# Transposing q and k in fp32 through two 64-row halves of the TensorE array

## The chip, the cores and the metric

The kernel runs on one NeuronCore of one Trainium2 chip. Its engines are TensorE (PE in the profile; PEld is its loading of weights), VectorE (DVE), ScalarE (ACT), GpSimd (POOL) and SyncE (SP), which here only issues DMAs. The metric is the device time of one execution in microseconds (us); lower is better. The two runs shown took 213.46 and 213.87 us, median 213.67 us.

## What is computed

Two blocks follow each other. The first is causal attention over 4 batches x 8 heads, 768 tokens, head size 64, in which each query sees only 6 chunks of 32 keys. The chunks are chosen by an upper bound on the scores:

```python
k_min = np.min(k_chunks, axis=3); k_max = np.max(k_chunks, axis=3)      # 24 chunks of 32 keys
ub = np.sum(np.maximum(q[:, :, :, None, :] * k_min[:, :, None, :, :],
                       q[:, :, :, None, :] * k_max[:, :, None, :, :]), axis=-1)
ub = np.where(causal, ub, -1000000000.0)
top_chunks = np.argsort(ub, axis=-1)[..., -6:]
scores = scale * np.matmul(q, k.transpose(0, 1, 3, 2))                 # kept where chosen and causal
attn = softmax(scores); out = np.matmul(attn, v)
```

The second is a gated feed-forward block on the 4 x 768 x 512 result `x`:

```python
h = gelu_tanh(x @ w_in); u, v = h[..., :512], h[..., 512:]
v_n = (v - mean(v)) / sqrt(var(v) + 1e-6) * g_ln
v_s = np.einsum('ts,bsd->btd', w_sg, v_n) + b_sg[None, :, None]
return x + (u * v_s) @ w_out
```

## The kernel before

**The pairs.** The 32 heads are handled as 16 pairs, p = 0 to 15; a pair's two heads (i = 0, 1) lie side by side, so that 128 partitions hold 2 x 64 features. Four pairs make a batch, and the feed-forward block of a batch (`moe_h`, `moe_g`) follows when its four pairs are done. While the pairs of one batch are scored, the pairs of the next are prepared.

**Preparing a pair** (`prep`, L1079) has these operations, under the names that the program gives them:

- `ktr` (L574): k arrives as 128 tokens x 128 (head, feature) in fp32, six such blocks. TensorE transposes each: the block is the stationary operand, an fp32 identity of 128 x 128 the moving one (`rows_T`, L547 to L553; the matmuls are on L550). Three blocks, one half (`hf`) of the 768 tokens, go into one PSUM bank as 128 x 384 fp32. A pair has two such operations.
- `kmm` (L578): VectorE reduces a bank to minimum and maximum over each 32 keys, 12 values per half. Two per half. `wsub` (L597) subtracts the minima from the maxima.
- `kev` (L585): the bank is copied as bf16 into `KA`, by ScalarE (by VectorE for pair 2). One copy per half for pairs 0 to 3 and 8 to 15, two copies of 64 partitions for pairs 4 to 7.
- `qtr` (L604), `qev` (L606): the same for q, two operations of three transposes, and one copy to `qT` in fp32 per half (VectorE for pairs 2 and 3). `rel` (L616) is a ReLU of `qT` (ScalarE from pair 4 on), `qcast` (L625) a cast to bf16 on GpSimd.
- `ub` (L660, L707): the bounds, 32 fp32 matmuls on tiles of 64 rows x 32 columns of the array, for one pair (p < 4) or two. Into two banks. Then `utr`, `m8`, `dn`, `dt` on VectorE pick the sixth largest bound and make the mask.

**Scoring a pair.** For pairs 0 to 3 `sc` (L834, L840) runs on tiles of 64 rows x 128 columns, one head in each half of the array's rows. From pair 4 on `sc` (L795) uses the whole array. `exp` (L801, L849) is ScalarE's exponential of up to 1024 columns. `pv` and `pvd` (L879, L885) multiply with v, `xs` (L897) scales the result. `xtr` (L919) transposes the attention's output for the feed-forward block, whose TensorE operations are `hv` (L943), `hu` (L962), `pt` (L1014) and `ou` (L1047); `os` (L1056) adds x on VectorE.

**PSUM.** There are eight banks of 2 KB per partition. Two pairs of banks (`PSC`) serve the scores alone; four single banks (`PSG`, slots 0 to 3) serve all else. From pair 6 on, `ktr`, `qtr` and `ub` may use slots 0 and 1 only (L558, L603, L695); `pv` has slots 2 and 3 (L875); `hv` and `hu` of the first three batches use all four (L939, L958). An operation that takes a slot waits for every operation on the slot's previous tile (L114 to L120), and operations of different engines on one tile wait for each other (L69 to L71).

**The order.** Every engine works through a fixed list. `Program.op` numbers the operations as the program text creates them; `TABLE` (L1133) holds, for each engine, the numbers in the order in which it issues them, further the slot of each PSUM tile, and `filler`: how many idle matmuls (L381, of a zero tile, to keep TensorE at work) it issues ahead of the wait of a given operation. The table was found by a search ahead of time; its costs are the functions at L232 to L258. TensorE's list is in order: an operation that waits for a slot holds up all that stand behind it. SP's queue of DMAs has such a list too.

Of the kernel before, what the change touches and what calls it, by code (L numbers as in the profile page):

```python
# [256 lines left out]
def dmac(issue=530):  # L257
    return issue, issue  # L258


def _build(nc, ctx, q, k, v, w_in, g_ln, w_sg, b_sg, w_out, out):
# [18 lines left out]
    TG = S // 2  # L280
# [42 lines left out]
    WSB = 1  # L323
    WSC = "pool"
# [152 lines left out]
    def wsg_load(j):  # L477
# [4 lines left out]
        if WSB:  # L482
# [3 lines left out]
            elif WSC == "dve":  # L486
                P.op("dve", lambda d: d.tensor_copy(sb, dst), dve(S, rate=2), ("wsc", j), port=True,
                     reads=[("stg", j % 4)] + names, writes=[("stb", j % 4)])
            else:
                P.op("act", lambda d: d.activation(sb, dst, ACTF.Copy), act(S), ("wsc", j),  # L490
                     reads=[("stg", j % 4)] + names, writes=[("stb", j % 4)])
            t = ps_g.tile((0, 1))
# [61 lines left out]

    def kside(p):
        s, w = p % NKS, p % NW
# [33 lines left out]
        if p >= KSPR:  # L590
            P.op("sp", lambda e: e.dma_start(KA[w][1][64:128, :], KA[w][0][64:128, :]), dmac(640), ("kcp", p),
                 reads=[("KA", w, 0, h) for h in range(2)], writes=[("KA", w, 1, h) for h in range(2)] + [("KI", w, 0)],
                 dma=f"kcp{w}", xfer=450)
            P.op("sp", lambda e: e.dma_start(KA[w][0][64:128, :], INDF[64:128, :]), dmac(640), ("kin", p),
                 reads=["INDF"], writes=[("KI", w, 0)], dma=f"kin{w}", xfer=450)
        ws = [("W", w, m, hf) for m in range(2) for hf in range(2)]
        P.op("dve", lambda d: d.tensor_tensor(W[w][:, 1, 0:NC], W[w][:, 1, 0:NC], W[w][:, 0, 0:NC],  # L597
                                              op=ALU.subtract), dve(24), ("wsub", p), port=True, reads=ws, writes=ws)
# [513 lines left out]
    for p in range(4, NP + 4):  # L1112
# [152 lines left out]
```

## Time and profile before

| what | us |
|---|---|
| median of the two runs (213.46, 213.87) | 213.67 |
| the profiled execution's own time | 213.85 |
| its span, first to last instruction | 212.1 |
| TensorE matmuls busy | 203.4 |
| VectorE busy | 184.1 |
| ScalarE busy | 158.5 |
| GpSimd busy | 88.8 |

The span is 1.75 us shorter than the execution's own time, for what lies before the first and after the last instruction. Busy times count the union of an engine's instructions. A matmul's record runs from its issue to the modelled end, about 0.16 us after its last column went in, so records of matmuls that follow each other overlap, and a short gap of TensorE hides in them. The granted clock of TensorE is 0.999 over the span.

### The profile page before, as it was taken

To read this page: it belongs to the slowest core of one execution; us is meant where nothing else is said; L and a number is where in the kernel's file an instruction comes from. 1 tells how busy PE (TensorE), PEld (TensorE's weight loads), DVE (VectorE), ACT (ScalarE), POOL (GpSimd) and SP (SyncE) were. 2 spreads that over 40 slices of the span, in tenths; PEclk is the share of its full clock that TensorE was granted. 3 is DMA by queue.
4 is the path that set the end of the run, shared out by engine and by line. 5 is a ranking of instruction groups with operands and counts; after the bars stand their busy time and mean duration, and the time that the engine had idled before them with its cause. 6 is when DMAs were issued, how large, how long until landed. Compare 5 with 4: busy or idle time off the path is not lost.

```text
span 212.1 us, 5923 instructions
## 1 busy us (share of the span) xinstructions
PE 203.4 (96%) x2326; PEld 134.0 (63%) x2326; DVE 184.1 (87%) x537; ACT 158.5 (75%) x246; POOL 88.8 (42%) x119
## 2 busy tenths in 40 slices
PE   7989999889999999999999999999999999999993
PEld 3646677644767577776456767779646668545552
DVE  2999999879999899898799999899897887788894
ACT  2468999987599779998949989999977868256000
POOL 8424697795262645474121456465502311002000
PEclk9999999999999999999999999999999999999999
DMA  7999999992989998898989988826320007412007
GB/s 152 218 219 254 212 237 336 338 306 68 221 225 231 215 273 205 194 211 189 230 201 220 207 165 220 224 79 149 59 61 3 3 0 97 129 47 105 2 33 264
DMA packets 91339, 36.07 MB, mean 170 GB/s; under 512 B 84144, under 2 KB 86448, under 8 KB 91312
## 3 DMA queue, kind: packets, MB, share of 16 engines
q1 hardware_dynamic: 91024, 35.31, 73.7%
q8 instruction: 18, 0.29, 0.6%
q10 hardware_dynamic: 288, 0.39, 0.5%
q14 instruction: 9, 0.07, 0.1%
HBM read 24.77 MB, written 6.29 MB: 146 GB/s over the span
## 4 chain that ended last, share of the span: by engine, by line
PE 63%; DVE 23%; ACT 9%; issue 2%; POOL 1%; DVEq 0%
PE PSG L1014 15%; PE PSC L795 11%; PE PSG L1047 9%; PE PSG L943 7%; DVE W L578 6%; PE PSG L962 6%; ACT E L801 5%; PE PSG L550 5%; PE PSG L879 4%; DVE vhat L996 3%; DVE XS L897 2%; PE PSG L707 2%; ACT KA L450 2%; PE PSC L382 2%; PE PSG L885 2%
## 5 line engine op out<-in xcount | busy, mean ns | idle before, releaser
L801 ACT ACTIVATE E<-PSC 128x1024 bf16<-128x1024 f32 (+1 forms) x72 | 62.9, 917 | 7.8 <-PE PSC L795 7.6
L795 PE MATMUL PSC<-QA,KA 128*128 128x128 bf16 (+2 forms) x336 | 37.5, 246 | 0.4
L578 DVE TENSOR_REDUCE W<-PSG 128x12 f32<-128x384 f32 x64 | 32.7, 547 | 3.8 <-PE PSG L550 3.6
L1014 PE MATMUL PSG<-wsgT,vhat 128*128 128x384 bf16 x192 | 34.5, 326 | 0.4 <-DVE vhat L996 0.2
L806 POOL TENSOR_SCALAR_AFFINE_SELECT E<-E 128x768 bf16<-128x768 bf16 x24 | 21.1, 878 | 32.3 <-ACT E L801 31.9
L625 POOL CAST QA<-qT 64x768 bf16<-64x768 f32 (+1 forms) x28 | 24.1, 859 | 15.9 <-ACT qT L450 10.0
L795 PEld LDWEIGHTS PSC<-QA,KA 128*128 128x128 bf16 x336 | 24.1, 98 | 8.4 <-ACT E L801 2.4
L1014 PEld LDWEIGHTS PSG<-wsgT,vhat 128*128 128x128 bf16 x192 | 17.9, 98 | 12.5 <-ACT uT L968 1.3
L1047 PE MATMUL PSG<-woutb,uT 128*128 128x512 bf16 (+1 forms) x100 | 23.7, 371 | 0.0
L962 PE MATMUL PSG<-xT,winb 128*128 128x384 bf16 x128 | 23.6, 326 | 0.0
L1031 DVE SCALAR_TENSOR_TENSOR PSG<-PSG,glnT,bsgbc 128x384 f32<-128x384 f32 x32 | 19.7, 619 | 4.1 <-PE PSG L1014 3.9
L849 ACT ACTIVATE E<-PSC 128x1024 bf16<-128x1024 f32 (+3 forms) x26 | 21.2, 866 | 2.4 <-PE PSC L840 2.1
L943 PE MATMUL PSG<-winb,xT 128*128 128x512 bf16 x96 | 22.1, 379 | 0.6 <-issue 0.6
L968 ACT ACTIVATE uT<-PSG 128x384 bf16<-128x384 f32 x32 | 15.1, 490 | 10.0 <-PE PSG L962 9.7
L450 ACT ACTIVATE KA<-PSG 128x384 bf16<-128x384 f32 (+1 forms) x38 | 18.3, 492 | 3.7 <-DVE W L578 3.3
L879 PE MATMUL PSG<-vx,E 128*128 128x65 bf16 x480 | 19.9, 194 | 1.0 <-DVE XS L897 0.6
L635 POOL CAST vx<-vn 128x768 bf16<-128x768 f32 x16 | 13.3, 836 | 17.8 <-DMA vn<-in_v_dram 13.4
L879 PEld LDWEIGHTS PSG<-vx,E 128*128 128x128 bf16 x480 | 17.6, 97 | 3.6 <-DVE XS L897 1.5
L948 ACT ACTIVATE vgb<-PSG 128x512 f32<-128x512 f32 x24 | 13.2, 599 | 7.2 <-PE PSG L943 7.0
L1035 DVE TENSOR_TENSOR uT<-PSG,uT 128x384 bf16<-128x384 f32 x32 | 17.7, 555 | 0.9
L897 DVE TENSOR_TENSOR XS<-PSG,rden 128x384 bf16<-128x384 f32 x32 | 17.7, 554 | 0.9
L952 DVE BATCH_NORM_STATS2 stats<-vgb 128x6 f32<-128x512 f32 x24 | 15.8, 685 | 2.6 <-ACT vgb L948 2.5
(88 smaller groups left out, 328.8 us busy)
## 6 DMA issues: line engine op xcount, KB each, us to landing
kn<-in_k_dram SPq DMA_DIRECT2D x32, 192.0 KB, 4.6
qn<-in_q_dram SPq DMA_DIRECT2D x32, 192.0 KB, 4.5
vn<-in_v_dram SPq DMA_DIRECT2D x12, 384.0 KB, 5.2
out_dram<-osb SPq DMA_DIRECT2D x18, 256.0 KB, 2.4
vn<-in_v_dram SPq DMA_DIRECT2D x8, 192.0 KB, 4.8
uT<-in_moe_w_sg_dram SPq DMA_DIRECT2D x4, 384.0 KB, 6.2
vgb<-in_moe_w_in_dram SPq DMA_DIRECT2D x3, 512.0 KB, 6.1
KA<-INDF SPq DMA_DIRECT2D x12, 96.0 KB, 2.6
```

Source lines behind the costliest of these rows:

```text
L450: P.op("act", lambda e: e.activation(dst(), src(), ACTF.Copy), act(n), tag, reads=reads, writes=writes, ps=ps, shift=shift)
L578: P.op("dve", lambda d, m=m, op=op, src=src, h0=h0, h1=h1: d.tensor_reduce(W[w][:, m, 12 * h0:12 * h1].rearrange("p (h c) -> p h c", h=h1 ...
L625: P.op("pool", lambda g, i=i, r0=r0, r1=r1: g.tensor_copy(QA[w][i or 0][r0:r1, :], qT[r][r0:r1, :]), gps(S, 250 if i == 1 else 150), ("qca ...
L795: r = e.matmul(t.ap()[:, o:o + n], KA[w][i][:, 128 * kb:128 * kb + 128], QA[w][i][:, q0:q0 + n], start=True, stop=True)
L801: P.op("act", lambda e, t=t, c0=c0, c1=c1, i=i: e.activation(E[es][:, i, c0:c1], t.ap()[:, 0:c1 - c0], ACTF.Exp, scale=SCALE), act(c1 - c0 ...
L849: P.op("act", lambda e, t=t, c0=c0, c1=c1, n=n: e.activation(E[es][:, :, c0:c1], t.ap().rearrange("p (i x) -> p i x", i=2)[:, :, 0:n], ACT ...
L879: r = e.matmul(t.ap()[:, 65 * (qb - q0):65 * (qb - q0) + 65], E[es][:, i, at[kb, qb]:at[kb, qb] + 128], vx[w][:, kb, i, :], start=x == 0, ...
L897: P.op("dve", lambda d, pv3=pv3, nq=nq, rs=rs, q0=q0, q1=q1: d.tensor_tensor(XS[:, b % 2, hh // 2, q0:q1, i * DH:(i + 1) * DH], pv3()[:, : ...
L943: r = e.matmul(t.ap()[:, 0:F], xT[s][:, dk, 128 * qt:128 * qt + 128], winb[:, dk, F:DFF], start=(dk == 0), stop=(dk == NDK - 1), skip_grou ...
L962: r = e.matmul(t.ap()[:, 0:TG], winb[:, dk, 128 * fb:128 * fb + 128], xT[s][:, dk, TG * tg:TG * tg + TG], start=(dk == 0), stop=(dk == NDK ...
L1014: r = e.matmul(t.ap()[:, 0:TG], vhat[s][:, sb, 128 * fb:128 * fb + 128], wsgT[:, sb, TG * tg:TG * tg + TG], start=(sb == 0), stop=(sb == N ...
L1047: r = e.matmul(t.ap()[:, 0:n1 - n0], gT[s][:, fb, 128 * qt:128 * qt + 128], woutb[:, fb, n0:n1], start=(fb == 0), stop=(fb == NF - 1))
```

## The change

In place of two operations of three transposes there is one of twelve. A block of 128 tokens is cut in two halves of 64 tokens, which lie on partitions 0 to 63 and 64 to 127. Each half is the stationary operand (64 rows x 128 columns) of a transpose of its own, with an identity of 64 x 64 as the moving operand, so that it occupies one half of the array's rows. The half r goes into bank r: a bank now holds, for each of the six blocks, its 64 tokens r, and not three whole blocks. The readers follow: `kmm` writes its 12 values in steps (two of every four), and the copies to `KA` and `qT` write runs of 64 tokens, every second one (`by64`, `flat64`). Sizes and number of the reductions, the copies and the DMAs are as before.

`ktr` and `qtr` each take two slots at once and each is marked done when its last transpose is done. There are 32 TensorE operations fewer in the list (405 before, 373 after), so all numbers are new, and the table is new too, from a search of 12 seconds. `WSD` is off and does nothing.

```diff
@@
+    WSD = 0
+    TR2 = 1
@@
+    def rows_T2(src, ts):
+        def tr(e):
+            for j in range(NT):
+                for r in range(2):
+                    res = e.matmul(ts[r].ap()[:, 64 * j:64 * j + 64],
+                                   src[64 * r:64 * r + 64, j].rearrange("p i d -> p (i d)"),
+                                   identF[64 * r:64 * r + 64, 64 * r:64 * r + 64], is_transpose=True)
+            return res
+        return tr
+
+    def by64(ap, r):
+        return ap.rearrange("p (j r x) -> p j r x", r=2, x=64)[:, :, r, :]
+
+    def flat64(ap):
+        return ap[:, 0:TG].rearrange("p (j x) -> p j x", x=64)
+
+    def kside2(p):
+        s, w = p % NKS, p % NW
+        ts = [ps_g.tile((0, 1, 2, 3) if p < 6 else (0, 1)) for _ in range(2)]
+        P.op("pe", rows_T2(kn[s], ts), pe32(*[64] * NT), ("ktr", p, 0), mode=1,
+             reads=[("kn", s, h, i) for h in range(2) for i in range(2)] + ["identF"], writes=ts, alloc=tuple(ts))
+        for h, t in enumerate(ts):
+            for m, op in ((0, ALU.min), (1, ALU.max)):
+                P.op("dve", lambda d, m=m, op=op, t=t, h=h: d.tensor_reduce(
+                    W[w][:, m, 0:NC].rearrange("p (j r c) -> p j r c", r=2, c=2)[:, :, h, :],
+                    t.ap()[:, 0:TG].rearrange("p (j c x) -> p j c x", c=2, x=32), axis=AX.X, op=op),
+                    dve(TG), ("kmm", p, h, m), reads=[t, ("W0", w)], writes=[("W", w, m, h)], ps=[t])
+            for i in (None,) if p < HALF or p >= KSPR else range(2):
+                r0, r1 = (0, 128) if i is None else (64 * i, 64 * i + 64)
+                evac("dve" if p in KDVE else "act", lambda h=h, i=i, r0=r0, r1=r1: by64(KA[w][i or 0][r0:r1, :], h),
+                     lambda t=t, r0=r0, r1=r1: flat64(t.ap()[r0:r1]), TG, ("kev", p, h), [t],
+                     [("KA", w, i or 0, h)] + ([("KI", w, 0)] if p >= KSPR else []), [t], shift=(i == 1))
+        kcopies(p, w)
...
     def kside(p):
+        if TR2:
+            kside2(p)
+            return
...
     def qside(p):
         s, w, r = p % NQS, p % NW, p % NR
+        if TR2:
+            ts = [ps_g.tile((0, 1, 2, 3) if p < 6 else (0, 1)) for _ in range(2)]
+            P.op("pe", rows_T2(qn[s], ts), pe32(*[64] * NT), ("qtr", p, 0), mode=1,
+                 reads=[("qn", s, h, i) for h in range(2) for i in range(2)] + ["identF"], writes=ts, alloc=tuple(ts))
         for hf in range(2):
+            if TR2:
+                t = ts[hf]
+                evac("dve" if p in QDVE else "act", lambda hf=hf: by64(qT[r][:], hf), lambda t=t: flat64(t.ap()), TG,
+                     ("qev", p, hf), [t], [("qT", r, hf)], [t])
+                continue
...
     "filler": (
-        "45:7 54:4 84:4 "),
+        "45:8 53:5 78:6 59:1 "),
```

`kcopies` holds, unchanged, the two DMAs and the subtraction that stood at the end of `kside` (L590 to L598). With the numbers written as names (pair, and half where there are halves), these stretches of the lists matter below. TensorE's new list after batch 0's third `ou`, and again in batch 1:

```
ub.6 sc.5.1.1 sc.4.1.2 ou.0.0  qtr.8  ou.0.5  qtr.10 ktr.9  pv.4.1 pvd.4.1 ou.0.4 pv.4.0 pvd.4.0  qtr.9  ou.0.3 sc.6.0.0  ktr.8
sc.11.0.1  qtr.15  pvd.9.1 sc.11.1.0 pvd.9.0 sc.11.1.2  ktr.14  sc.11.1.1 sc.11.0.0 ou.1.3 ou.1.5 pv.10.0 pvd.10.0 sc.12.0.0  ktr.15
```

The old list has at the first of these places: `ou.0.0 qtr.10.1 sc.4.0.2 ou.0.5 qtr.8.0 sc.4.1.2 qtr.10.0 sc.5.1.2 qtr.8.1 sc.5.1.1 qtr.9.0 ktr.9.0 ou.0.4 ...`. ScalarE's new list at the first place: `qev.8.1 qev.8.0 rel.8 qev.10.0 qev.10.1 rel.10 kev.9.0 kev.9.1 qev.9.1 qev.9.0 rel.9 exp.6.0.0`. VectorE's at the second: `rcp.9.1 kmm.14 xs.9.1 rcp.9.0 kmm.14 xs.9.0 kmm.14 os.1.3 kmm.14 os.1.5`. At the start of the attention of batch 0 VectorE's new list has one of the copies of `IND` (L412) ahead of the first reduction. Ahead of `ub.4` and batch 0's feed-forward block, three of the four `xtr` of that batch now stand before `ub.4`; in the old list two of the four did.

Counted over TensorE's whole list, neighbouring operations change between the array whole, in 64 x 128 tiles and in 64 x 32 tiles 49 times before and 76 times after. Up to and into `ub.4` there are 38 such changes before and 27 after; behind it 11 and 49, for the ten pairs 6 to 15 have 20 transposing operations there, of which only `qtr.10` and `ktr.9` are neighbours.

More of the change, by code (lines that the diff above doesn't have):

```diff
@@ L491, in wsg_load @@
                      reads=[("stg", j % 4)] + names, writes=[("stb", j % 4)])
+            if WSD:
+                P.op("sp", lambda e: e.dma_start_transpose(wsgT[:, :, 128 * j:128 * j + 128], sb), dmac(1300), ("wst", j),
+                     reads=[("stb", j % 4)] + [("vhat", 0, x) for x in range(NT)],
+                     writes=[("wsgT", j, hf) for hf in range(2)], dma=f"wt{j}", xfer=900)
+                return
             t = ps_g.tile((0, 1))
@@ new lines, in kcopies @@
+    def kcopies(p, w):
+        if p >= KSPR:
+            P.op("sp", lambda e: e.dma_start(KA[w][1][64:128, :], KA[w][0][64:128, :]), dmac(640), ("kcp", p),
+                 reads=[("KA", w, 0, h) for h in range(2)], writes=[("KA", w, 1, h) for h in range(2)] + [("KI", w, 0)],
+                 dma=f"kcp{w}", xfer=450)
+            P.op("sp", lambda e: e.dma_start(KA[w][0][64:128, :], INDF[64:128, :]), dmac(640), ("kin", p),
+                 reads=["INDF"], writes=[("KI", w, 0)], dma=f"kin{w}", xfer=450)
+        ws = [("W", w, m, hf) for m in range(2) for hf in range(2)]
+        P.op("dve", lambda d: d.tensor_tensor(W[w][:, 1, 0:NC], W[w][:, 1, 0:NC], W[w][:, 0, 0:NC],
+                                              op=ALU.subtract), dve(24), ("wsub", p), port=True, reads=ws, writes=ws)
@@ L589, in kside @@
                      [("KA", w, i or 0, h) for h in hs] + ([("KI", w, 0)] if p >= KSPR else []), ts, shift=(i == 1))
[L590 to L598, printed above, removed]
+        kcopies(p, w)
     def qside(p):
         s, w, r = p % NQS, p % NW, p % NR
+        if TR2:
+            ts = [ps_g.tile((0, 1, 2, 3) if p < 6 else (0, 1)) for _ in range(2)]
+            P.op("pe", rows_T2(qn[s], ts), pe32(*[64] * NT), ("qtr", p, 0), mode=1,
+                 reads=[("qn", s, h, i) for h in range(2) for i in range(2)] + ["identF"], writes=ts, alloc=tuple(ts))
         for hf in range(2):
+            if TR2:
[3 more added lines that the diff above has]
+                continue
             t = ps_g.tile((0, 1, 2, 3) if p < 6 else (0, 1))
```

9 lines of the change are left out of this document (5 added, 4 removed), and 116 rows, old and new, of the table TABLE.

## The prediction

> **What bounds the kernel now.** I read the page first (spans, shares, the chain of waits), then busy time in six stretches, for all and for the transposes alone, then single lines and tiles, last TensorE's timeline at a few places. From the page:
>
> ```profile
> span 212.1 us, 5923 instructions
> PE 203.4 (96%) x2326; PEld 134.0 (63%) x2326; DVE 184.1 (87%) x537; ACT 158.5 (75%) x246; POOL 88.8 (42%) x119
> ...
> PE 63%; DVE 23%; ACT 9%; issue 2%; POOL 1%; DVEq 0%
> ```
>
> TensorE has most of the chain, but not everywhere. The stretches (length; busy PE, PEld, DVE, ACT, POOL; clock, DMA) say where:
>
> ```profile
> 0.00:46.00 46.00, 41.74 (x648) 28.00 (x648) 38.88 (x126) 35.30 (x57) 30.75 (x52) 1.00 1.10 254
> 46.00:81.00 35.00, 34.73 (x278) 22.27 (x279) 32.75 (x101) 28.35 (x48) 18.08 (x23) 1.00 0.95 204
> 81.00:97.00 16.00, 15.36 (x268) 11.99 (x265) 14.47 (x51) 15.74 (x25) 9.80 (x13) 1.00 0.90 204
> 97.00:113.00 16.00, 15.77 (x139) 8.82 (x140) 13.91 (x39) 11.47 (x22) 2.84 (x3) 1.00 0.96 212
> 113.00:152.00 39.00, 39.00 (x544) 29.52 (x544) 35.46 (x115) 37.07 (x53) 20.65 (x25) 1.00 0.78 168
> ```
>
> From 81 to 97 ScalarE works 15.74 of 16 us and sets the pace. From 46 to 81 and from 113 on it is TensorE, with VectorE close behind. In the first 46 us VectorE has 38.88 us, and most of it is chain:
>
> ```profile
> 9.52 1.94 DVE W L578 x4
> ...
> 29.25 1.40 DVE W L578 x3
> ...
> 44.67 0.78 PE PSG L919 x12
> ```
>
> The fp32 transposes alone, in the same stretches (PE's busy time and count first):
>
> ```profile
> 0.00:46.00 46.00, 11.89 (x72) 8.23 (x72) 1.00 1.10 254
> 46.00:81.00 35.00, 6.63 (x42) 4.86 (x42) 1.00 0.95 204
> 81.00:97.00 16.00, 4.23 (x27) 2.87 (x27) 1.00 0.90 204
> 97.00:113.00 16.00, 2.08 (x12) 1.33 (x12) 1.00 0.96 212
> 113.00:152.00 39.00, 6.26 (x39) 4.53 (x39) 1.00 0.78 168
> ```
>
> 72 of 192 lie in VectorE's stage, 27 in ScalarE's, 93 where TensorE counts. The busy times overstate them, since records overlap. What one costs comes from its line and two places of the timeline:
>
> ```profile
> L550 PE MATMUL PSG<-identF,kn x96: 272/273/475, 4.6 to 145.8; 128*128 128x128 f32 x96
> ...
> 70.04 0.38 PE L550 MATMUL PSG<-identF,qn 128*128 128x128 f32 x2
> ...
> 70.20 0.66 PE PSG L550 x6
> ```
>
> A record is 272 ns, two take 0.38 us, so the second starts 109 ns after the first; six take 0.66 us of the chain, 6 x 109 = 654 ns.
>
> **The change part by part. Transposing.** A half block has 64 columns to move where the whole one had 128. 109 ns for 128 are 0.83 ns each and 2.5 over, so 64 take 56 ns if both halves run at once. That halves run at once is seen in the scores of pairs 0 to 3, which use the same tiles in bf16:
>
> ```profile
> 18.80 0.23 PE L834 MATMUL PSC<-QA,KA 64*128 64x128 bf16 x2
> ...
> L840 PE MATMUL PSC<-Dt,IND 64*128 64x128 bf16 x40 | 3.7, 216 | 0.0
> ```
>
> The two matmuls together take 0.23 us, one alone 216 ns. Nothing was loaded ahead for them, and both are longer by little more than 10 ns: the weights of the second half did not wait for the first's. So twelve transposes are six rounds. A round can't be shorter than the load of the next fp32 weights, which shows where none was loaded ahead:
>
> ```profile
> 18.99 0.33 PE L550 MATMUL PSG<-identF,kn 128*128 128x128 f32 x1
> ```
>
> 0.33 us against 272 ns: the load holds it up 56 ns. I take 57 ns a round (estimate from these two rows). The bounds are 56 and 112, the latter if the halves' loads go one after the other.
>
> The Trainium skill, "TensorE: Matmul & The Clock Gate", LDWEIGHTS (loading the stationary operand), says that a load takes its columns divided by 1.2 in ns, and that rows don't matter. A half block would then load as long as a whole one, 107 ns, and nothing would be gained; the 56 ns above speak against the size, but no run here shows an fp32 load of 64 rows and 128 columns.
>
> **Changing the tiling.** A price comes with it that the twelve have to pay:
>
> ```profile
> 73.42 0.40 PE L707 MATMUL PSG<-rT,W 64*32 64x288 f32 x1
> 73.76 0.39 PE L1047 MATMUL PSG<-woutb,uT 128*128 128x512 bf16 x1
> ```
>
> Within one tiling the next matmul starts 272 - 109 = 163 ns before the record of the last one ends. Here it starts 60 to 70 ns before (73.42 + 0.40 against 73.76): about 95 ns are lost. A `ktr` or `qtr` alone among whole-array operations pays 95 on entry, 56 for its first load, which can't be done ahead, 6 x 57 for the rounds, 95 on the way out and 11 for the next operation's bf16 load: 599 ns against 654. That is 55 ns saved, not 327. Behind `ub.4` there are 20 of them: 20 x 55 = 1.1 us, and 0.25 us more for the two neighbours, 1.35 us. Of the 120 transposes replaced there 93 lie where TensorE sets the time: **-1.05 us**.
>
> "TensorEngine Tiling (Array Packing)" of the Trainium skill, Overview, Theoretical Speedup, gives up to 2x for a contracted dimension of 64 or less. By that alone each operation would save 327 ns and the 93 some 5 us; the two changes and the first load measured above are what it leaves out.
>
> **The first 46 us.** There 72 transposes become 72 rounds, 72 x 52 = 3.7 us, and 11 changes of tiling fewer save 11 x 106 = 1.2 us (`ktr` and `qtr` now stand among scores of the same tiling). These 4.9 us lie beside VectorE, whose reductions and copies are as many and as long. What gets out is at the end: of the 0.78 us of `xtr` behind `ub.4` half the work now stands ahead of it. I take **-0.5 us**, between 0 and -4.9.
>
> **The start.**
>
> ```profile
> 1.25 3.60 PE L382 MATMUL PSC<-warm 128*128 128x512 bf16 x8 [1.25 <-DVE warm L379]
> 4.65 1.54 PE L550 MATMUL PSG<-identF,kn 128*128 128x128 f32 x6
> ...
> 5.66 1.59 DVE L578 TENSOR_REDUCE W<-PSG 128x12 f32<-128x384 f32 x3 [2.97 <-PE PSG L550]
> ```
>
> Eight idle matmuls end at 4.65; a ninth adds 0.43 us ((3.60 - 0.6) / 7). VectorE began when three transposes were done; now it needs all twelve, which at this slow rate (0.21 us apart) take about 0.65 us and a switch. It begins some 0.55 us later, and 0.35 us of that is filled with a copy of `IND` that it had to do anyway: **+0.2 us** (0 to +0.6).
>
> **The banks.** This is the part with the largest unknown. An operation takes both slots and waits until both are read out, and TensorE waits with it, with all that is behind: scores for ScalarE, `ou` and `pt` for VectorE. Before, one half's bank could be filled while the other was read. The price was small:
>
> ```profile
> PEld PSG L550 <- ACT qT L450: 1.1, 3, 0.4
> PEld PSG L550 <- DMA kn<-in_k_dram: 0.7, 1, 0.7
> ...
> PE PSG L550 <- ACT qT L450: 0.2, 1, 0.2
> ```
>
> A read-out of q is two copies, of k four reductions and a copy:
>
> ```profile
> L578 DVE TENSOR_REDUCE W<-PSG 128x12 f32<-128x384 f32 x64 | 32.7, 547 | 3.8 <-PE PSG L550 3.6
> L450 ACT ACTIVATE qT<-PSG 128x384 f32<-128x384 f32 x28 | 13.4, 497 | 0.9 <-PE PSG L550 0.6
> L616 ACT ACTIVATE rT<-qT 128x576 f32<-128x576 f32 x12 | 8.2, 691 | 0.1
> L897 DVE TENSOR_TENSOR XS<-PSG,rden 128x384 bf16<-128x384 f32 x32 | 17.7, 554 | 0.9
> L1056 DVE TENSOR_TENSOR osb<-PSG,XS 128x512 f32<-128x512 f32 x18 | 12.1, 682 | 1.2 <-PE PSG L1047 1.1
> ...
> 139.52 0.86 PE PSG L1047 x4
> ...
> 142.20 0.45 PE PSG L879 x15
> ```
>
> In the new list `ktr.9` stands right behind `qtr.10`. ScalarE still has `rel.8` (0.69, beside `qtr.10` itself) and two copies (0.99) to do, so with the hand-over TensorE stands about 1.1 us. Between `ktr.9` and `qtr.9` it has one `ou` and pair 4's `pv` and `pvd`, 0.86 + 2 x (0.45 + 0.19) = 2.1 us, while the banks need 4 x 0.547 + 0.5 + 0.2 = 2.9: 0.6 us. Between `ktr.14` and `ktr.15` there are 3.7 us of TensorE, and VectorE has four reductions, two `xs`, a reciprocal and an `os` in its list, 2.19 + 1.11 + 0.19 + 0.68 = 4.2, then a copy and the hand-over 0.6: 1.1 us. `ktr.14` behind `qtr.15` waits 0.3 more. The first two stand in ScalarE's stage, where TensorE has slack: I count 0.6 of their 1.7. With 1.4 from the others that makes **+2.0 us**, between 0 (TensorE gets there late anyway) and +5 (19 visits of 0.27 us).
>
> SP's queue issues the same DMAs in a slightly other order; loads of pairs 9 to 13 stand earlier in it. TensorE waits for a load once in the profile (0.7 us for the first k, above), so I cost it at nothing. The rest of the new order could be off by a microsecond either way; it has no row.
>
> **Sum.** 213.85 - 1.05 - 0.5 + 0.2 + 2.0 = **214.5 us**, against the profiled execution's own time; the median of the runs, 213.67, is 0.2 below it.
>
> **The rivals.** *Loads set the pace.* If the two halves' weights go in one after the other, a round is 112 ns, or 107 by the skill's rule above. The 93 rounds that count get 55 ns dearer, +5.1: 219.6 us. Against it speak the pair of scores above, in bf16. It decides from rounds of about 95 ns on. The same time results if the halves don't run at once at all, which would mean that the change doesn't do what it says.
>
> *The banks cost more.* If the 19 visits behind `ub.4` wait 0.4 us each, the longest such wait in the rows above, this is 7.6 us, of which 78% (93 of 120) count, 5.9 in place of 2.0: 218.4 us. It is slower by 2% from waits of 5.4 us in sum on. For it: VectorE is busy 35.46 of 39 us from 113 on, so reductions come late. Against it: `ktr` and `qtr` stand 2 to 6 us apart at most places.
>
> *The first stage follows TensorE.* If the 4.9 us freed there shorten it fully, and the waits for banks come to 0.5 us: 213.85 - 1.05 - 4.9 + 0.2 + 0.5 = 208.6 us. For it: TensorE's busy 41.74 of 46. Against it: the pieces of VectorE in the chain from 9.5 to 31 us.
>
> **How the numbers follow.** 2% (4.3 us) is about what a measurement of this kernel can tell from no change. The forecast has 0.72; loads 0.09; the banks 0.12, of which 0.08 above 217.9; the first stage 0.07, of which 0.05 below 209.4. So faster 0.05, within 2% 0.78, slower 0.17. The range takes the bounds of the start and the banks upward, and half of the first stage's downward: 210.8 to 218.8 us.
>
> **What would show it.** In TensorE's timeline a `ktr` should start its pairs about 57 ns apart and span 0.5 us (113 ns: the loads), with some 95 ns lost on either side. Idle time of L550 that ends on `qT` or `KA` of ScalarE should rise from 1.3 to several us, with `ktr.9` among the longest. Batch 0's feed-forward block should start 0 to 1 us before 46.06. I am wrong if that block starts 2 us or more earlier, if rounds take over 90 ns, or if L550's waits stay under 1 us.

## The result

The changed kernel took 226.66 and 228.11 us, median 227.38, against 213.67 before: a ratio of 1.0642, with a 95% interval of 1.049 to 1.0794. The same kernel repeated beside later experiments took 224.16 to 228.05 us, median 225.59 (1.0533, 1.0508 to 1.0559). Ratios leave out runs over 1.5% above the fastest, so the 228.05 us count in this median and not in its ratio. The forecast was 214.5, the range ended at 218.8.

The profiled execution took 228.11 us. From its page (first the span and the busy times, then the granted clock in 40 slices, then the chain of waits by engine):

```profile
span 226.1 us, 6300 instructions
...
PE 204.9 (91%) x2509; PEld 129.6 (57%) x2523; DVE 187.8 (83%) x537; ACT 160.4 (71%) x246; POOL 89.1 (39%) x119
...
PEclk9988999969999999999589999999999999999999
...
PE 58%; DVE 26%; ACT 10%; DMA 2%; issue 2%; POOL 1%; DVEq 0%; ACTq 0%
```

TensorE is busy about as long as before (204.9 against 203.4 us) in a span that is 14 us longer, so it idles where it did not; the clock has dips that the old profile hasn't; and DMAs, which had no share of the chain, have 2%. The stretches, with limits moved to the same events as before (length; busy PE, PEld, DVE, ACT, POOL; clock, DMA):

```profile
0.00:51.00 51.00, 42.19 (x731) 28.09 (x734) 40.22 (x125) 35.35 (x57) 33.17 (x54) 0.93 1.09 243
51.00:88.00 37.00, 34.85 (x331) 20.21 (x333) 33.99 (x103) 30.02 (x49) 16.73 (x21) 1.00 0.97 194
88.00:104.30 16.30, 13.96 (x262) 10.05 (x262) 14.36 (x53) 13.83 (x21) 8.30 (x10) 1.00 1.15 226
104.30:125.50 21.20, 17.87 (x172) 9.77 (x172) 13.28 (x33) 12.98 (x26) 4.64 (x5) 0.84 1.28 205
125.50:165.50 40.00, 39.12 (x576) 27.63 (x578) 36.70 (x111) 36.66 (x51) 19.29 (x23) 1.00 0.44 111
```

The first stretch is 5 us longer (it was 46 us), the second 2, the fourth 5.2 (it was 16, from 97 to 113); the others are level within a microsecond. Two places carry most of the loss: the first 51 us, and the start of batch 1's feed-forward block.

**The operations themselves** work as described. One of them alone among whole-array operations:

```profile
99.18 0.45 PE L853 MATMUL PSC<-QA,KA 128*128 128x256 bf16 x3
99.56 0.58 PE L568 MATMUL PSG<-identF,kn 64*128 64x64 f32 x12
100.10 0.28 PE L853 MATMUL PSC<-QA,KA 128*128 128x128 bf16 x2
```

Its rounds, from the same place, with two and with three pairs counted:

```profile
99.56 0.34 PE L568 MATMUL PSG<-identF,kn 64*128 64x64 f32 x4
99.56 0.40 PE L568 MATMUL PSG<-identF,kn 64*128 64x64 f32 x6
```

A record is 222 ns, so the second pair starts some 110 ns after the first, and the third 60 ns after the second. From the operation's first start to the next operation's are 0.54 us. Its first start lies 0.07 us ahead of the end of the record before it, where 163 ns are normal (the prediction's figure), so some 90 ns go on entry: about 0.63 us in all, against 0.654 for the two old ones together.

**The waits for banks.** The idle time ahead of L568 by what ended it (us, times), then the part of the matmuls alone (with the longest):

```profile
  ACT qT L452: 5.0, 9
  ACT KA L452: 4.7, 7
```

```profile
PE PSG L568 <- ACT KA L452: 2.0, 3, 1.3
PE PSG L568 <- ACT qT L452: 1.7, 3, 1.0
```

The first two rows add up to 9.7 us, but they count weight loads and matmuls each for itself, so a wait that holds up both stands in them twice. The matmuls stand 3.7 us in six waits (0.2 us in one before); three of the six, 1.65 us, lie behind the start of batch 0's block.

**The clock.** TensorE's clock fell to half for 3.41 us from 15.30 and from 46.02, and for 6.83 us from 107.46. These are steps of a fixed grid of 3.41 us. A step ahead of each fall, the steps at half clock, and last a step of the same grid that was followed by no fall (same columns as above):

```profile
11.89:15.30 3.41, 1.38 (x32) 1.17 (x34) 3.34 (x16) 1.40 (x4) 0.83 (x1) 1.00 1.35 220
15.30:18.71 3.41, 3.41 (x46) 1.67 (x40) 2.08 (x5) 1.86 (x3) 0.00 (x0) 0.50 1.04 198
42.61:46.02 3.41, 1.56 (x33) 1.13 (x30) 1.63 (x5) 3.37 (x6) 3.27 (x5) 1.00 1.06 259
46.02:49.43 3.41, 3.19 (x47) 3.01 (x55) 1.41 (x4) 2.42 (x5) 3.16 (x4) 0.50 1.09 299
104.05:107.46 3.41, 2.00 (x45) 1.60 (x45) 3.20 (x10) 2.27 (x6) 1.74 (x3) 1.00 1.69 230
107.46:110.87 3.41, 1.44 (x8) 0.84 (x9) 1.52 (x4) 0.86 (x2) 0.74 (x1) 0.50 0.78 133
110.87:114.29 3.42, 3.42 (x20) 1.56 (x19) 0.00 (x0) 2.08 (x3) 0.11 (x1) 0.50 1.27 224
86.98:90.40 3.42, 1.90 (x38) 1.22 (x35) 3.29 (x9) 0.98 (x2) 0.00 (x0) 1.00 1.08 299
```

Ahead of each fall TensorE was busy 2.00 us of a step or less. But 1.90 us were enough to be followed by none, so the covered share alone doesn't decide. The step with 2.00 has 24 of the half transposes among its 45 matmuls, that with 1.90 has none; whether that is the reason no run shows. The Trainium skill, "TensorE: Matmul & The Clock Gate", Part 1 (the HAM clock gate), lets the clock fall after a window of some 3.4 us that is idle, and says that the window runs freely. The grid agrees, but here no window was idle: ahead of one fall, records covered 59% of it.

**Batch 1's feed-forward block.** SP's queue, then TensorE, at the place (start, length of the row; what a wait ended on in brackets):

```profile
99.52 2.39 SPq L964 DMA_TRANSPOSE xT<-XS  x1
101.96 0.58 SPq L535 DMA_DIRECT2D kn<-in_k_dram  x1
102.58 0.54 SPq L1121 DMA_DIRECT2D out_dram<-osb  x1
103.17 0.43 SPq L535 DMA_DIRECT2D kn<-in_k_dram  x1
103.64 0.65 SPq L600 DMA_DIRECT2D KA<-KA  x1
104.33 1.35 SPq L964 DMA_TRANSPOSE xT<-XS  x1
```

```profile
107.89 0.82 PE L977 MATMUL PSG<-identB,XS 128*128 128x128 bf16 x6 [1.64 <-ACT KA L452]
110.25 1.06 PE L1001 MATMUL PSG<-winb,xT 128*128 128x512 bf16 x2 [1.54 <-DMA xT<-XS]
```

Two loads of pair 13, a store and a copy stand in SP's queue between the transposes of pairs 5 and 6 (`xtd.1.1`, `xtd.1.2`). The latter is issued at 104.33 and lands 5.47 us later in the chain of waits, with the loads under way beside it. Ahead of that, `xtr.1.3` waits for the bank that `ktr.11` holds.

### The profile page after: what moved, and what is told of

Its sections match the earlier page's. It is cut to its first block, busy times and chain, and to the rows that moved or that the text cites. A ratio compares the mean times of both kernels' runs of the same rounds, so it can differ in the third digit from the quotient of the medians.

```text
span 226.1 us, 6300 instructions
## 1 busy us (share of the span) xinstructions
PE 204.9 (91%) x2509; PEld 129.6 (57%) x2523; DVE 187.8 (83%) x537; ACT 160.4 (71%) x246; POOL 89.1 (39%) x119
## 4 chain that ended last, share of the span: by engine, by line
PE 58%; DVE 26%; ACT 10%; DMA 2%; issue 2%; POOL 1%; DVEq 0%; ACTq 0%
PE PSG L1072 12%; PE PSC L853 8%; PE PSG L1105 8%; DVE W L587 6%; PE PSG L1001 5%; PE PSG L937 4%; PE PSG L1020 4%; ACT E L907 4%; PE PSG L568 3%; DVE stats L1010 3%; PE PSG L765 3%; DVE m L785 3%; DVE U L774 3%; DMA xT<-XS 2%; DVE vhat L1054 2%
## 5 line engine op out<-in xcount | busy, mean ns | idle before, releaser
L853 PE MATMUL PSC<-QA,KA 128*128 128x128 bf16 (+2 forms) x336 | 38.0, 246 | 0.8 <-ACT E L859 0.7
L587 DVE TENSOR_REDUCE W<-PSG 128x12 f32<-128x384 f32 x64 | 32.2, 547 | 1.3 <-PE PSG L568 1.0
L853 PEld LDWEIGHTS PSC<-QA,KA 128*128 128x128 bf16 x336 | 23.6, 98 | 10.2 <-ACT E L859 3.6
L1001 PE MATMUL PSG<-winb,xT 128*128 128x512 bf16 x93 | 23.3, 399 | 1.8 <-DMA xT<-XS 1.5
L1020 PE MATMUL PSG<-xT,winb 128*128 128x384 bf16 x128 | 23.1, 326 | 0.0
L1105 PE MATMUL PSG<-woutb,uT 128*128 128x512 bf16 (+1 forms) x90 | 21.2, 370 | 0.4
L1042 POOL TENSOR_TENSOR rstd<-rstd,neghalf 128x6 f32<-128x6 f32 x4 | 5.3, 1329 | 33.7 <-DVE rstd L1040 33.7
```

Source lines behind the costliest of these rows:

```text
L587: P.op("dve", lambda d, m=m, op=op, t=t, h=h: d.tensor_reduce(W[w][:, m, 0:NC].rearrange("p (j r c) -> p j r c", r=2, c=2)[:, :, h, :], t. ...
L853: r = e.matmul(t.ap()[:, o:o + n], KA[w][i][:, 128 * kb:128 * kb + 128], QA[w][i][:, q0:q0 + n], start=True, stop=True)
L1001: r = e.matmul(t.ap()[:, 0:F], xT[s][:, dk, 128 * qt:128 * qt + 128], winb[:, dk, F:DFF], start=(dk == 0), stop=(dk == NDK - 1), skip_grou ...
L1020: r = e.matmul(t.ap()[:, 0:TG], winb[:, dk, 128 * fb:128 * fb + 128], xT[s][:, dk, TG * tg:TG * tg + TG], start=(dk == 0), stop=(dk == NDK ...
L1105: r = e.matmul(t.ap()[:, 0:n1 - n0], gT[s][:, fb, 128 * qt:128 * qt + 128], woutb[:, fb, n0:n1], start=(fb == 0), stop=(fb == NF - 1))
```

## The experiments

All ratios are to the kernel before, run beside them (213.56 to 213.83 us).

**Which part: operations or lists?** Four kernels cross the two. The first keeps the new lists and puts six whole transposes into each merged operation:

```diff
             for j in range(NT):
-                for r in range(2):
-                    res = e.matmul(ts[r].ap()[:, 64 * j:64 * j + 64],
-                                   src[64 * r:64 * r + 64, j].rearrange("p i d -> p (i d)"),
-                                   identF[64 * r:64 * r + 64, 64 * r:64 * r + 64], is_transpose=True)
+                res = e.matmul(ts[j // 3].ap()[:, 128 * (j % 3):128 * (j % 3) + 128],
+                               src[:, j].rearrange("p i d -> p (i d)"), identF[:], is_transpose=True)
```

> The changed kernel with its lists, its merged operations and its two banks each, but each ktr and qtr does six whole 128 x 128 transposes (three per bank) in place of twelve half ones. If the row halves are what costs 13.7 us (changes of tiling, rounds of loads), this gives 213 to 217 us. If the cost lies in the merged operations or the new lists, TensorE has 0.65 in place of 0.6 us per operation and more work in the stages where it idles: 224 to 229 us, and TensorE's clock may fall less often.

227.13 us (1.0637, 1.0602 to 1.0672): level with the changed kernel.

The second has the old operations, two of three whole transposes with a bank and an end of their own, in the new lists and slots:

```diff
-TensorE's list: ... ktr.9 ...
+TensorE's list: ... ktr.9.0 ktr.9.1 ...     (so for all 32; the old program otherwise)
```

> The kernel before (two operations of three whole transposes, one bank each) with the new lists and slots: each merged operation of the new list is replaced by its two halves, one behind the other. If the new lists cost the time, 222 to 229 us. If the merging does (both banks free at once, both released at once), 213 to 217 us, since a half starts as soon as its own bank is free.

226.45 us (1.0609, 1.0585 to 1.0633). The lists alone, without any changed operation, cost 12.9 us. Its idle time ahead of the transposes that ends on `qT` or `KA` is 3.5 us, not 9.7 (weight loads and matmuls both counted), and this gains almost nothing: what comes late in these lists is late by other waits too.

The third and fourth have merged operations in the old lists, each at the place of its second half, with 28 entries moved where the lists could not run otherwise; one with whole transposes, one with row halves:

```diff
-TensorE's list: ... qtr.10.1 sc.4.0.2 ou.0.5 qtr.8.0 sc.4.1.2 qtr.10.0 ...
+TensorE's list: ... sc.4.0.2 ou.0.5 sc.4.1.2 qtr.10 ...
```

> Merged operations of six whole transposes in two banks, with the lists of the kernel before: each stands where the later of its two halves stood, and 28 operations of the other engines were moved by one to three places, for the lists to be able to run. If the merging costs the time, 219 to 226 us. If the new lists do, 213 to 217 us.

> The change with the lists of the kernel before, mended as in the run of six whole transposes: merged operations, row halves. If the row halves cost time, 3 us or more above that run; by the prediction's sum for TensorE (55 ns saved per operation behind ub.4, more ahead of it) up to 2 us below it. If the new lists are at fault 212 to 216 us, if the merging is, 219 to 226 us.

264.33 us (1.2366, 1.2331 to 1.24) and 261.88 (1.2251, 1.222 to 1.2281), far above all that was expected. So the old order can't be kept with all 32 operations merged at these places: it interleaves the halves of several pairs. With both held to one order, row halves are 2.45 us faster than whole ones.

**What does one merged operation cost in the old order?** Only `ktr.15` is merged, at the place of its first half:

```diff
-... ktr.14.1 sc.11.0.2 ktr.15.0 ou.1.3 pv.10.0 ... sc.12.1.0 ktr.15.1 pv.11.1 ...
+... ktr.14.1 sc.11.0.2 ktr.15 ou.1.3 pv.10.0 ... sc.12.1.0 pv.11.1 ...
```

> The old lists, untouched, with one operation of 32 merged into row halves: k of pair 15, at the place of its first half. The old list has the two halves 5 us apart, with pv, scores and an ou between. If a bank that is asked for early is what costs (TensorE stands there until VectorE has read the bank's last tile, and all behind it stands too), one merged operation adds 3 to 5 us: 216.5 to 218.5 us. Rival, the bank is a matter of a microsecond and the rest of the lists takes it up: 213.5 to 214.7 us.

217.67 us (1.0174, 1.0156 to 1.0192), as expected of the bank: 3.9 us for one of 32 operations. One of the four runs kept its clock full (1.0; the others 0.992) and took 216.62 us; by that one run some 2.8 us are the bank's and about 1 us the clock's. TensorE at the place:

```profile
139.71 0.49 PE L557 MATMUL PSG<-identF,kn 128*128 128x128 f32 x3
140.04 0.44 PE L853 MATMUL PSC<-QA,KA 128*128 128x256 bf16 x3
142.81 0.59 PE L568 MATMUL PSG<-identF,kn 64*128 64x64 f32 x12 [2.33 <-ACT KA L452]
143.33 1.34 PE L1105 MATMUL PSG<-woutb,uT 128*128 128x512 bf16 x4
```

and the waits of the ten microseconds around it (us in total, times, longest):

```profile
DVE osb L1114 <- PE PSG L1105: 2.7, 2, 2.5
PEld PSG L568 <- ACT KA L452: 2.6, 1, 2.6
```

`ktr.15` stands until `ktr.14`'s second bank has been reduced by VectorE and copied by ScalarE, 2.33 us. `ou.1.3` stands behind it, and VectorE, which has to add x to its result (`os`), waits for that 2.5 us: the two engines wait for each other in turn. The clock then falls to half for 3.41 us.

Merged where the banks are free, the operations do no such harm. The old lists again, with 12 operations merged at places that a model of the lists' costs showed as free:

```diff
-ktr.p.0 and ktr.p.1 for p = 0 to 5, 12; qtr.p.0 and qtr.p.1 for p = 0, 2, 4, 6, 13
+ktr.p, qtr.p, at the place of the half that stood first
```

> The old lists, untouched, with 12 of the 32 transposing operations merged into row halves (k of pairs 0 to 5 and 12, q of 0, 2, 4, 6, 13), each at the place of its first half: those at which, by the costs, both banks are free when it comes. If holding two banks costs only where one of them is still in use, this is level or a little faster: 12 operations save 55 ns or more each where TensorE counts, 212.8 to 213.8 us. Rival, merged operations cost something wherever they stand: 215 us or more.

214.82 us (1.005, 1.0033 to 1.0067). It came out between the two: no gain, and half a per cent lost. Nine of the 12 stand ahead of batch 0's block, where the prediction has TensorE's savings beside VectorE, so this says little of what row halves gain behind it.

**The clock.** The changed kernel with idle matmuls of the zero tile into a free score bank ahead of five operations that wait:

```diff
+        def fill(e, t=t, n=n):
+            for _ in range(n):
+                r = e.matmul(t.ap()[:, 0:512], warm[:, 0:128], warm[:], start=True, stop=True, skip_group_check=True)
+            return r
```

> The changed kernel, its order kept, with 26 idle matmuls of the zero tile ahead of five waiting operations (6 ahead of sc.0.2, 5 ahead of qtr.5, 1 ahead of wst.5, 7 ahead of xtr.1.3, 7 ahead of hv.1.4), so that TensorE streams in the stretches that came ahead of the half clock. If the half clock is a cause of its own: the three stretches of 13.65 us at half clock cost at most 6.8 us of work, part of it beside waits, so 221 to 224.5 us and no clock step after the first 10 us. Rival, the half clock only marks waits that would last as long anyway: 226 to 228 us with the clock full.

223.87 us (1.0475, 1.0452 to 1.0497), clock 1.0 from 4.6 us on. Stretches that hold the second and the third fall (the last two hold what was at half clock from 107.46 to 114.29):

```profile
36.00:50.00 14.00, 12.63 (x231) 8.22 (x226) 10.40 (x34) 12.44 (x19) 11.50 (x15) 1.00 1.05 301
...
106.00:110.00 4.00, 4.00 (x29) 1.93 (x28) 0.13 (x1) 1.74 (x3) 0.00 (x0) 1.00 1.32 218
110.00:114.00 4.00, 4.00 (x23) 1.88 (x21) 2.17 (x6) 3.99 (x8) 0.83 (x1) 1.00 1.24 208
```

How much that is depends on what it is held against, so the changed kernel was run again:

```diff
 (the changed kernel, unaltered)
```

> The changed kernel once more, as it is, beside the next run: its windows of the clock lie elsewhere in each execution, so that its times may spread. If the clock's windows hit it by chance: 224 to 228 us with a spread of over 1 us. If its three stretches of half clock are always there: 226.5 to 228.

225.59 us, with a spread of 3.9 us; its profile has two falls, from 44.13 and 108.99, and steps of 1.93 and 1.92 us that were followed by none. The grid lies elsewhere in the two profiles, and the same waits hit it or not. The clock's share is 1.7 us against this median and 3.5 against the first; about 10 us remain with the clock full.

**SP's queue.** One entry of the changed kernel's list moved:

```diff
-SP's list: ... kn.11.1 xtd.1.1 kn.13.1 st.0.3 kn.13.0 kcp.9 xtd.1.2 kcp.8 ...
+SP's list: ... kn.11.1 xtd.1.1 xtd.1.2 kn.13.1 st.0.3 kn.13.0 kcp.9 kcp.8 ...
```

> The changed kernel with one entry of SP's list moved: xtd.1.2, the DMA transpose of pair 6's output for batch 1's feed-forward block, stands right behind xtd.1.1, ahead of the two loads kn.13, a store and kcp.9. Theory, SP's queue: TensorE waits for that transpose from 106 to 110; it would be issued 2.4 us earlier at most (when xs.6 is done, 1.4 us earlier) and land without the two loads beside it, 2.7 us less: 3 to 4 us, and the half clock behind it goes, up to 2 us more: 222 to 224.5 us. Rival, something else is late by as much there (the copy to KA of ktr.11, the reductions): 226.5 to 228 us.

224.38 us (1.0506, 1.0457 to 1.0554): 3.0 below the first median of the changed kernel, 1.2 below the second, whose runs (224.16 to 228.05) overlap with these (223.84 to 226.13). The wait for `xT` is gone from the profile; what is last now is the copy to `KA` of `ktr.11`, ahead of `xtr.1.3`, and the clock still falls to half there, for 6.8 us from 103.7:

```profile
PE PSG L977 <- ACT KA L452: 1.6, 1, 1.6
```

Both mends at once:

```diff
+the idle matmuls of the kernel above
+SP's list: xtd.1.2 right behind xtd.1.1
```

> The changed kernel with both mends at once: the idle matmuls that hold the clock up (3.5 us alone) and xtd.1.2 ahead of the loads of pair 13 (3.0 us alone against the changed kernel's time). If they are two causes: 220.5 to 222.5 us. If both mend the same stretch (104 to 114 us), 223.5 to 224.5.

224.39 us (1.0501, 1.0483 to 1.052): no sum. With the clock held, the moved entry gains nothing (223.87 without it). They mend the same stretch, or the one's gain lies within what the grid gives or takes.

**Where in the lists?** The old lists up to and into `ub.8`, the new ones behind it, with the old operations:

```diff
 each engine's list: what the old list issues up to ub.8, in the old order
+then the rest in the new order
```

> Separate whole transposes as before; all five lists are the old ones up to and into ub.8 (batch 0 and its feed-forward block done), the new ones from there on. If the new order loses at separate places (4 to 6 us in the first 46, 2 to 3 up to 85, 5 to 6 at 99 to 106), only the last is left: 218.5 to 220.5 us. Rival, the loss is one thing that runs through the new lists, wherever they are used, in proportion to their length: 213.6 + 12.9 x 0.6 = 221.3 or more; or it starts in the first 46 us and runs on: under 216.

224.11 us (1.0493, 1.046 to 1.0526): above the theory's 220.5 and within the rival's "221.3 or more", but not for the rival's reason, since the loss isn't spread over the lists. By matching VectorE's and ScalarE's instructions of both traces, it is level with the old kernel at `xs.7` (-0.1 us) and 10.2 us late at batch 1's last `gv`; from there to the end it loses 1.4 us more. One place costs it 10 us:

```profile
95.00:101.00 6.00, 4.01 (x64) 3.09 (x63) 5.76 (x14) 4.35 (x9) 2.18 (x4) 1.00 1.17 240
101.00:108.00 7.00, 1.59 (x5) 0.85 (x6) 1.07 (x2) 0.33 (x1) 1.39 (x2) 0.53 1.03 209
```

```profile
100.45 0.51 PE L919 MATMUL PSG<-identB,XS 128*128 128x128 bf16 x6 [1.65 <-ACT KA L450]
106.41 1.46 PE L943 MATMUL PSG<-winb,xT 128*128 128x512 bf16 x3 [5.45 <-DMA xT<-XS]
```

TensorE's list has nothing ahead of the block that could run, so it waits 5.45 us for the transpose by DMA and goes on at half clock (a mean of 0.53 in the row above). How much of the 10 us is the clock's, this run doesn't separate. Mended there:

```diff
-SP's list: ... st.0.5 qn.13.1 qn.13.0 st.0.4 vn.11 qn.12.1 xtd.1.0 xtd.1.1 kn.13.1 st.0.3 kn.13.0 xtd.1.2 kcp.8 ...
+SP's list: ... st.0.5 xtd.1.0 qn.13.1 qn.13.0 xtd.1.1 st.0.4 vn.11 qn.12.1 xtd.1.2 kn.13.1 st.0.3 kn.13.0 kcp.8 ...
-VectorE's list: ... kmm.11.0 kmm.11.0 kmm.11.1 kmm.11.1 wsub.11 xev.1.3 ...
+VectorE's list: ... kmm.11.0 kmm.11.0 xev.1.3 kmm.11.1 kmm.11.1 wsub.11 ...
```

> The run with the old lists up to ub.8 and the new ones behind, which loses 10.2 us between xs.7 (level with the old) and batch 1's first gv, with this one place mended: in SP's list the three transposes xtd.1.0, xtd.1.1, xtd.1.2 each ahead of the loads and stores that stood before them (qn.13, st.0.4, kn.13), and in VectorE's xev.1.3 ahead of the second half of kmm.11. Theory, the loss is this queue at this place: 215 to 218 us. Rival, the new lists lose at this place in any case, for TensorE's order has nothing to do while batch 1's last pair is finished: 220 us or more.

222.14 us (1.0385, 1.0361 to 1.0409). 2.0 us come back, and the wait for `xT` is 2.0 us in place of 5.45; the rest stays, as the rival had it. Its reason, that the new order has no other work for TensorE while pair 7 is finished, fits but wasn't tried: no run gave TensorE other work there.

**Is it the short search?** Lists from a longer search, by moves of entries and slots over the kernel's own cost functions, with the clock's grid. First for the changed program and for the old one alike:

```diff
-TABLE of 12 seconds
+TABLE of some 27 minutes
```

> The changed program as it is (row halves, two banks at once), with an order from a search of some 27 minutes in place of 12 seconds, started from the list of 12 seconds, over a model of costs with the granted clock in it. Theory, the list is what costs and the operations do not: under 213.6 us, about 205 to 211. Rival, holding two banks at once costs and no order makes up for it: 218 us or more.

> The control: the old operations (separate whole transposes), started from the old list, with the same search for the same time. If merging with row halves is even (55 ns saved an operation, banks held longer), within 2 us of the run with row halves; if row halves pay by their term, 1 to 3 us above it; if holding two banks costs, 5 us or more below it.

247.81 us (1.1585, 1.1497 to 1.1672) and 252.39 (1.1846, 1.1776 to 1.1917), both far worse and no test of anything but the costs. The profile of the first shows what these left out. ScalarE loads its function tables 26 times, against 8 before, for the search had mixed exponentials and GELUs; 12 of them stand ahead of the exponentials:

```profile
L859 ACT ACT_TABLE_LOAD x12 | 15.4, 1283 | 0.2
```

and a copy of VectorE within SBUF stood behind GpSimd. One line's copies (shortest, median and longest, ns), then the longest of them, then GpSimd at the time:

```profile
L807 DVE COPY KA<-INDF x4: 495/595/3158, 31.1 to 49.3; 64x768 bf16<-64x768 bf16 x4
```

```profile
44.15 3.16 DVE L807 COPY KA<-INDF 64x768 bf16<-64x768 bf16 x1
```

```profile
44.10 2.02 POOL L448 CAST winb<-vgb 128x1024 bf16<-128x1024 f32 x2
46.06 1.04 POOL L448 CAST winb<-xT 128x1024 bf16<-128x1024 f32 x1
```

The copy ends 0.2 us after the third cast, in GpSimd's first pause. Two others of the four copies, at 31.12 and 49.31, ran beside two casts and took 0.66 and 0.53 us.

With both in the costs, the search was made again for both programs:

```diff
-TABLE of 12 seconds (the changed program), TABLE of before (the old one)
+TABLE of 28 minutes
```

> The changed program (row halves, two banks) with an order from a second search, 28 minutes, whose costs now hold what the first run of this kind showed to be missing: 1.28 us for each change of ScalarE's function tables, and VectorE's copies waiting for GpSimd's instruction. Theory, the order is what costs: under 213.6 us (the costs say 5 us below those of the old kernel in the same terms). Rival, holding two banks at once costs: 216 us or more, and at least 3 us above the separate operations ordered in the same way.

> The control: the old operations (whole, separate) with an order from the same second search, started from the old list. The costs say 7.7 us below the old list and 2.5 below the row halves. If row halves are worth their term with an order of their own, this run is 1 us or more above that of the row halves; if two banks at once cost more than that, 2 to 5 us below it. Against the old list: 206 to 213 us if the costs hold, over 214 if they miss something again.

223.11 us (1.0429, 1.0406 to 1.0452) for row halves, clock full, and 215.36 (1.0075, 1.0055 to 1.0096) for the old operations. So the merged operations end 7.75 us behind the separate ones. That is no equal test: the search for row halves started from the list of 12 seconds (225.59 us), that for the old operations from the old list (213.76 us), and it ended above its start, so these costs still miss something. The old operations searched for from the list of 12 seconds were not run.

Two last runs took the row halves out of that order (six whole transposes in the merged operation), and let the search go on for 25 minutes more:

```diff
 first run, in the order of 28 minutes:
-for r in range(2): res = e.matmul(ts[r]... 64 rows ...)
+res = e.matmul(ts[j // 3]... 128 rows ...)
 second run, with row halves:
-TABLE of 28 minutes
+TABLE of 53 minutes
```

> The order of the second search for row halves (223.1 us there, clock full throughout), with six whole 128 x 128 transposes in each merged operation in place of the twelve of 64 rows; both banks are held as before. It leaves the rounds and the changes of tiling as the only difference. By the prediction's terms, row halves save 55 ns an operation alone and some 150 to 330 where the neighbours are 64-row scores: 1 to 4 us slower than with row halves, 224 to 227 us. Rival, the order takes it up: within 0.7 us.

> Row halves, the same search run on for another 25 minutes from where the second stopped; the costs say 1.4 us less. If the search was what was short, 219 to 222 us; if a floor of the two-bank operation is reached, 222 to 224 us.

225.93 us (1.0553, 1.0515 to 1.0592): without the row halves, the same order is 2.8 us slower. And 220.16 us (1.0275, 1.0231 to 1.032): still 6 us behind the old kernel, but 3 better than the search before. No run here is faster than the kernel before.

## Why the prediction was wrong

- **Rounds, 57 ns.** The duration is right, for the time from the second start on: 0.58 us for twelve, less a record of 222 ns and a first step of 110, leaves four rounds of about 60. But the second pair of a visit starts 110 ns after the first, which the terms did not hold. An operation alone costs 0.63 us at the place shown, not 0.599, and the 55 ns saved shrink to some 20. The rival "loads set the pace" is out.
- **The -1.05 us.** Right in sign. In one fixed order row halves were worth 2.45 and 2.8 us; in the new lists of the change, nothing that shows (227.13 for whole ones). The 2.8 were measured in an order that had been searched for row halves.
- **The first 46 us, -0.5.** Wrong in sign. Batch 0's block starts at 50.9 instead of 46.1 us. With the clock held it starts at 47.8 (second row), and at 47.5 in the run with `xtd.1.2` moved, whose clock did not fall before it. So some 3 us of the 4.8 lie in the clock, and the rival by which this stage gets 4.9 us shorter is out:

```profile
L1001 PE MATMUL PSG<-winb,xT x93: 378/379/634, 50.9 to 202.4; 128*128 128x512 bf16 x93
L1001 PE MATMUL PSG<-winb,xT x96: 377/379/390, 47.8 to 197.6; 128*128 128x512 bf16 x96
```

- **The start, +0.2.** The last reduction of pair 0 ends 0.1 us later than before.
- **The banks, +2.0.** The mechanism was right and so was one place: `ktr.9` behind `qtr.10` waits 0.97 us in the row below, where 1.1 was worked out. the matmuls of `ktr.15`, for which 1.1 was worked out too, did not wait; the 0.6 us for `qtr.9` should by its own terms be 2.9 - 2.1 = 0.8. In sum the size was near: behind the start of batch 0's block TensorE's matmuls stand 1.65 us for banks. But these waits are not what the change costs: with the old operations in the same order they come to 1.2 us of the matmuls instead of 3.7, and the time is the same. So the rival "the banks cost more" (218.4) isn't borne out in these lists either. What the sum of waits leaves out is who waits for the operations behind them. In the experiment with `ktr.15`, 2.33 us of waiting become 2.8 us with the clock full and 3.9 with the half clock that follows.

```profile
86.03 0.58 PE L568 MATMUL PSG<-identF,kn 64*128 64x64 f32 x12 [0.97 <-ACT qT L452]
```

- **"SP's queue ... I cost it at nothing".** Incomplete. That loads of pairs 9 to 13 stand earlier was seen, but the other transfers in that queue were not followed: the transposes by DMA that feed the next block stand behind these loads, and TensorE waits 1.54 us for one. What the one entry is worth isn't clear of noise: 3.0 us against the first median, 1.2 against the second, nothing with the clock held.
- **"The rest of the new order could be off by a microsecond either way; it has no row."** This is the step that decided. The old operations in the new order take 12.9 us longer, without any changed operation, so the order is what costs. Nor could the old one simply be kept: with all 32 operations merged at the places of their second halves it takes 48 to 51 us longer. The change needs an order in which a pair's two banks come free together, and all three searches for one ended above the old kernel. Whether two banks at once force that price, or the searches and their start do, is not shown.
- **The clock** was in no term: 1.7 to 3.5 us. The profile before had it at full speed, and I didn't ask what gaps would do to it. It falls behind steps in which TensorE waited, so it is a part of the new order's price.
- **The range.** Its ends don't follow from the bounds named for it. With the start at +0.6 and the banks at +5 the sum is 217.9, or 218.4 with nothing from the first stage, not 218.8; with half the first stage's 4.9 it is 212.6, not 210.8. The measured time lies above all of these.

What would show it: rounds and the waits that L550's line had came out as written (9.7 us in the counting that gave 1.3, so "several"), and batch 0's block starting late was outside both the forecast and the condition that was named as making it wrong, which looked only to the early side.

What stays open: whether an order exists in which row halves win. The last search was still gaining, 220.16 us against 223.11; that for the separate operations had the better start. Of the time that the lists cost with the clock full, by matched instructions of the run with idle matmuls, some 4.5 us have arisen by `xs.7`, 8.3 by batch 1's last `gv` and 9 to 10 at the end; in the first stretch no entry was tried alone.

## What to carry to other kernels

An operation that takes two buffers at once, where two operations took one each, changes more than its own time: it has to be placed where both are free, so ask which entries stand between the halves now, and what becomes of them. When a change brings a new order with it, the order is a part of the change and has to be costed: run the old operations in the new order, which separates the two at once. And follow every transfer in a queue that is reordered to the one that needs it, not only the ones that were moved ahead.

## What the runs showed of the hardware

- TensorE's clock fell to half for whole steps of a 3.41 us grid, without an idle step ahead. In the thirteen profiles in which it fell ahead of the end, every step at full clock in which TensorE's records covered 1.56 us or less was followed by one at half clock, and none with 2.2 us or more was. Between these, some were (2.00 and 2.18 us among them) and others not (1.90 and 1.93). The grid's place differed between the two profiles of the same program; its six runs took 224.16 to 228.11 us at granted clocks of 0.97 to 0.992.
- A change of ScalarE's function table takes 1.28 us each time.
- A copy of VectorE within SBUF took 3.16 us in place of 0.5 while GpSimd went from one cast to the next without a pause; two others beside two casts took 0.66 and 0.53 us. The Trainium skill, "SBUF — State Buffer", Terms, says that the port pair the two share is exclusive and that the loser blocks fully. The 3.16 us agree, over three casts in a row; the two shorter copies show no such wait.
- Row halves of fp32 transposes do run at once, in rounds of about 60 ns after a first of 110; a change of tiling cost some 90 ns on entry at the place shown.
